# A windowed attention with a SoLU layer: the row scale only in the halves of s, a fixed order on VectorE, a shared transpose of the last 64 columns, x first of the loads

## The chip, the cores and the metric

The kernel runs on one core of a Trainium2 chip. The core has five engines that run side by side, each through its own queue in order: TensorE (PE, with its weight loads as PEld), VectorE (DVE), ScalarE (ACT), GpSimd (POOL) and SyncE (SP, which here only issues DMAs). The metric is the device time in microseconds (us); lower is better. Matmuls write to PSUM, from which DVE and ACT read; POOL works in SBUF alone.

## The reference

Two stages run one after the other. The first is an attention over a window of 7 tokens whose weights are given: a softmax over the 7 taps, then a weighted sum of the current token and the 6 before it, separately for 8 heads of 24 columns. The second is a layer with a SoLU activation and a layer norm, on each of the 8 × 4160 = 33280 tokens:

```
w = exp(weight_gen - max_k)
w = w / (sum_k w + 1e-9)                          # 33280 tokens x 8 heads x 7 taps
x = sum_k w[..., k] * x_pad[t + k]                # 33280 x 192

h = x @ w_in                                      # 192 -> 1024
e = exp(h - max(h))
solu = h * e / (sum(e) + 1e-9)
ln = (solu - mean(solu)) / sqrt(var(solu) + 1e-6) * g_ln
out = ln @ w_out                                  # 1024 -> 192
```

A factor per row that multiplies solu cancels in the layer norm, apart from the small 1e-6; the kernel makes use of that.

## The kernel before

**Tiling.** The tokens are laid out so that each of the 128 partitions owns a run of 260 consecutive tokens; "tile t" is token t of every partition, so a tile is 128 tokens and there are 260 tiles. `starts` cuts the run into chunks (4, 8 and 4 tiles, then 16 each) for the loads, and attention works on groups of 4 tiles (the first two groups have 2).

**The stages of a tile**, with the names that the order uses:

- `att` (`attend`, `attention`): POOL multiplies x by the tap weights (tile `pr`) and adds the seven products partly, leaving two or three partial sums in `half` (`rows_left`). `fin` (`last_sum`) adds the rest on DVE into `a`, and `dup` (`copy_columns`) has ACT copy columns 128 to 191 once more, so that each token has 256 columns in `a`.
- For a pair of tiles, `xT` (`transpose_x`) transposes with four matmuls against the identity into one PSUM tile `pa`: columns 0 to 127 of each token, and columns 128 to 191, twice over, of each token. The first product works with x as a sum of a rounded part and its rest, so `xhi` (`high_x`) rounds `pa` on ACT, `xn` (`subtract_high`) subtracts the rounded part in PSUM with two matmuls against `minus` (the second subtracts only in the lower 64 rows), and `xlo` (`low_x`) copies the rest. For one pair of four (`on_vector`) `xld` (`low_x_on_vector`) has DVE do this in place of `xn` and `xlo`.
- `mm1` (`first_product`) is h = x w_in, ten matmuls into one of three PSUM tiles `h`: three terms with the 128 leading rows and two with the last 64, where the rounded part and its rest fill 128 rows.
- `max`, `vb`, `vr` on DVE: the negated row maximum, a bound that is no less than half of one, and its reciprocal (the row scale SIGMA). `exp` on ACT gives e and its row sum Z. `solu` on DVE writes h × SIGMA × e over h, with the row sum M. `sq` on ACT gives the sum of the squared deviations. `hi` and `lo` write s = h × 2^14 as two half-precision parts (ACT, then DVE), `tr` transposes both with a DMA from SP, and `mm2` (`second_product`) multiplies them with w_out in 24 matmuls. `out` scales on ACT, and `od` stores four tiles at a time.
- `f0` to `f7` (`scales`) work out the last row factor for a group of four tiles by small steps that alternate between ACT and DVE: f0 adds 1e-9 to Z, f1 multiplies by SIGMA, f2 squares, and f3 to f7 form the reciprocal root.
- `t0` to `t6` (`softmax_taps`) are the softmax over the taps of a chunk, on DVE, POOL and ACT in turn.

**The preparation.** w_in and w_out come as 64-bit numbers and are turned into pairs of shorter ones by steps on DVE, ACT and PE (`a..`, `b..` for w_in, `c..`, `q..`, `p..` for w_out), in PSUM tiles that the loop needs later. SP issues the loads of weight_gen's first chunk, then of x's first chunk (L79) and its eight halos (L81), the second weight_gen chunk, w_out, g and x's second chunk; ACT's queue issues the four loads of w_in.

**What sets the order.** All operations of all tiles are put in one order by a planner at build time. `plan` lists each operation with its engine, an assumed duration and what it waits for; `issue_order` plays this through and takes, on each free engine, the operation with the least tile number plus an offset from the table URGENCY, among those that are ready within PATIENCE. Some entries have a `ready` time, before which they aren't placed. The result is a fixed instruction stream for each engine: at run time an engine stands still when its next instruction isn't ready, even if one behind it is.

Of the kernel before, what the change touches and what calls it, by code (L numbers as in the profile page):

```python
# [29 lines left out]
def tile_kernel(ctx: ExitStack, tc: tile.TileContext, x, weight_gen, w_in, w_out, g_ln, out):  # L30
# [39 lines left out]
    def load_x(c, part=0):  # L70
# [5 lines left out]
        if c == 0:  # L76
# [3 lines left out]
            for b in range(B):  # L80
                nc.sync.dma_start(  # L81
                    xv[b * PB + 1 : (b + 1) * PB, :HALO, :],
                    x_run[b * PB : (b + 1) * PB - 1, RUN - HALO :, :],
                )
# [102 lines left out]
    minus = const.tile([P, 2, P], F32R, name="minus")  # L187
    nc.vector.tensor_scalar_mul(minus[:, 0], ident, -1.0)
    nc.vector.tensor_scalar_mul(minus[:D2, 1], ident[:D2], 0.0)
    nc.vector.tensor_scalar_mul(minus[D2:, 1], ident[D2:], -1.0)  # L190
# [197 lines left out]
    def columns(t):  # L388
        return a_of[t // TG][:, t % TG : t % TG + group(t), :]

    def last_sum(t):
        if t % TG == 0:

            a_of[t // TG] = att.tile([P, TG, 2 * P], F32, name="a", bufs=3)
        half = half_of.pop(t)
        nc.vector.tensor_reduce(  # L396
            columns(t)[:, :, :D], half.rearrange("p j t d -> p t d j"), axis=AX.X, op=ALU.add
        )

    def copy_columns(t):  # L400
        a = columns(t)
        nc.scalar.copy(a[:, :, D:], a[:, :, P:D])
# [4 lines left out]
    def transpose_x(t):  # L407
        a = a_of[t // TG]
        pa = ps_a.tile([P, 2, 2, P], F32, name="pa")

        for i in range(2):
            for n in range(2):
                nc.tensor.matmul(  # L413
                    pa[:, n, i, :], a[:, (t + i) % TG, n * P : (n + 1) * P], ident,
                    is_transpose=True, start=i == n == 0, stop=i == n == 1,
                )
        x_parts[t] = [pa]

    def high_x(t):
        hi = small.tile([P, 2, 2, P], F32R, name="x_hi", bufs=2)  # L420
        nc.scalar.copy(hi, x_parts[t][0])  # L421
        x_parts[t].append(hi)

    def subtract_high(t):

# [1 line left out]
        for n in range(2):
            nc.tensor.matmul(
                pa[:, n], minus[:, n], hi[:, n], start=False, stop=n == 1, skip_group_check=True
            )  # L430

    def low_x(t):
        pa, hi = x_parts.pop(t)
        lo = small.tile([P, 2, 2, P], F32R, name="x_lo", bufs=2)
        nc.scalar.copy(lo, pa)  # L435
        for i in range(2):
            xt_of[t + i] = hi[:, 0, i, :], lo[:, 0, i, :], lo[:, 1, i, :]

    def low_x_on_vector(t):

        pa, hi = x_parts.pop(t)
        lo = small.tile([P, 2, 2, P], F32R, name="x_lo", bufs=2)
        for out, n, rows in ((lo, 0, slice(None)), (hi, 1, slice(D2, P))):
            nc.vector.tensor_tensor(
                out=out[rows, n], in0=pa[rows, n], in1=hi.bitcast(F32)[rows, n], op=ALU.subtract
            )
        for i in range(2):
            xt_of[t + i] = hi[:, 0, i, :], lo[:, 0, i, :], hi[:, 1, i, :]
# [41 lines left out]
    def solu(t):  # L490
        h, e = h_of[t], e_of[t]
        nc.vector.scalar_tensor_tensor(  # L492
            out=h, in0=h, scalar=stat(t, SIGMA), in1=e, op0=ALU.mult, op1=ALU.mult, accum_out=stat(t, M)
        )
# [8 lines left out]
    def high_half(t):  # L503
        hl = hl_of[t] = big.tile([P, 2, FF], F16, name="hl", bufs=3)
        nc.scalar.activation(hl[:, 0, :], h_of[t], AF.Copy, scale=2.0**14)  # L505

    def low_half(t):
        hl = hl_of[t]
        nc.vector.scalar_tensor_tensor(  # L509
            out=hl[:, 1, :], in0=h_of[t], scalar=2.0**14, in1=hl[:, 0, :],  # L510
# [10 lines left out]
    def scales(t, step):  # L521
# [9 lines left out]
        if step == 0:  # L531
            nc.scalar.activation(of(ZE), of(Z), AF.Copy, bias=1e-9)
        elif step == 1:
            reduce(U, ZE, 2, ALU.mult)
        elif step == 2:
            nc.scalar.activation(of(E), of(U), AF.Square, scale=1e-3 * FF**1.5)
# [363 lines left out]
```

## Time and profile before

| | us |
|---|---|
| median of 3 runs | 1310.42 |
| lowest and highest run | 1307.23, 1311.84 |
| the profiled execution | 1309.91 |
| its span, first to last instruction | 1308.1 |

The granted TensorE clock of the profiled execution is 0.994 over the span. The costliest groups of each engine, by source line:

| line | engine | what | count | busy us | mean ns |
|---|---|---|---|---|---|
| L135 | POOL | products of taps and x, four tiles | 64 | 621.5 | 9711 |
| L561 | PE | second product | 6192 | 557.4 | 247 |
| L492 | DVE | solu | 260 | 333.5 | 1283 |
| L509 | DVE | second half of s | 260 | 317.7 | 1222 |
| L473 | DVE | row maximum | 260 | 316.8 | 1218 |
| L498 | ACT | squares | 260 | 293.7 | 1130 |
| L413 | PE | transposes of x | 520 | 80.4 | 276 |
| L428 | PE | subtraction of the rounded part | 196 | 47.2 | 322 |

Busy time is the time in which at least one instruction of the group runs. Instructions of one engine overlap at their ends, so the mean duration is longer than the step from one start to the next. The first product starts at 27.96 us, since its first transposes wait for the first `fin`, which starts at 24.22.

### The profile page before, as it was taken

What the parts mean: (1) busy time and instruction counts of PE and PEld (TensorE: products, weight loads), DVE (VectorE), ACT (ScalarE), POOL (GpSimd) and SP (SyncE); (2) the same over time, 40 slices, a digit from 0 to 9 for tenths busy, and PEclk for the clock granted to TensorE, in tenths of its full rate; (3) what the DMA queues carried; (4) which work ended last, traced back from release to release, by engine and by line L of the source; (5) the groups of instructions that cost most, each with busy time, mean ns of one, the idle gap of its engine ahead of it and who ended that gap; (6) DMA issues with size and microseconds to landing.
All of it is one profiled execution on the core that took longest, in us unless ns stands there. A gap on an engine that the chain in (4) does not pass through costs nothing.

```text
span 1308.1 us, 25825 instructions
## 1 busy us (share of the span) xinstructions
PE 1239.4 (95%) x9574; PEld 1069.3 (82%) x9574; DVE 1247.9 (95%) x2055; ACT 1151.4 (88%) x2271; POOL 1195.8 (91%) x243
## 2 busy tenths in 40 slices
PE   1689999999999999999999999999999999999998
PEld 1577788788888888888888888888888888888887
DVE  6889999999999999999999999999999999999995
ACT  5778888899899989989898989989898998998896
POOL 6999989999999999999999999999999999999910
PEclk9899999999999999999999999999999999999999
DMA  8488658697787969777796987788797876975665
GB/s 236 87 184 181 144 130 175 136 203 140 165 174 144 212 127 204 140 174 167 151 205 132 199 143 167 170 162 189 137 203 141 176 165 141 199 140 119 132 139 130
DMA packets 565917, 211.35 MB, mean 162 GB/s; under 512 B 544552, under 2 KB 545960, under 8 KB 565792
## 3 DMA queue, kind: packets, MB, share of 16 engines
q1 hardware_dynamic: 565344, 208.14, 76.3%
q10 hardware_dynamic: 448, 1.57, 0.5%
q8 instruction: 75, 1.23, 0.4%
q14 instruction: 50, 0.41, 0.1%
HBM read 46.15 MB, written 25.56 MB: 55 GB/s over the span
## 4 chain that ended last, share of the span: by engine, by line
DVE 51%; ACT 24%; issue 16%; PE 7%; DMA 2%; ACTq 0%; SPq 0%; DVEq 0%
DVE h L492 19%; DVE stats L473 15%; ACT e L486 9%; DVE a L396 8%; ACT e L498 5%; ACT hl L505 5%; PE h L459 3%; PE po L561 3%; ACT x_hi L421 2%; DVE hl L509 2%; ACT ot L572 2%; DVE stats L477 2%; DVE wm L114 1%; DVE wm L122 1%; DVE stats L529 1%
## 5 line engine op out<-in xcount | busy, mean ns | idle before, releaser
L135 POOL TENSOR_TENSOR pr<-xt,wt 128x5376 f32<-128x5376 f32 (+1 forms) x66 | 631.4, 9567 | 10.2 <-DMA wt<-in_weight_gen_dram 7.5
L561 PE MATMUL po<-w_hl,hlT 128*128 128x192 f16 x6192 | 557.4, 247 | 13.6 <-ACT ot L572 11.7
L561 PEld LDWEIGHTS <-hlT 128*128 128x128 f16 x6240 | 513.9, 98 | 61.6 <-issue 55.4
L492 DVE SCALAR_TENSOR_TENSOR h<-h,stats,e 128x1024 f32<-128x1024 f32 x260 | 333.5, 1283 | 4.5 <-ACT e L486 4.4
L509 DVE SCALAR_TENSOR_TENSOR hl<-h,hl 128x1024 f16<-128x1024 f32 x260 | 317.7, 1222 | 6.6 <-ACT e L498 2.9
L473 DVE TENSOR_REDUCE stats<-h 128x1 f32<-128x1024 f32 x260 | 316.8, 1218 | 3.7 <-PE h L459 3.0
L486 ACT ACTIVATE e<-h,stats 128x1024 f32<-128x1024 f32 x260 | 292.2, 1124 | 19.1 <-DVE stats L473 10.4
L498 ACT ACTIVATE e<-h,stats 128x1024 f32<-128x1024 f32 x260 | 293.7, 1130 | 7.0 <-DVE hl L509 5.7
L505 ACT ACTIVATE hl<-h 128x1024 f16<-128x1024 f32 x260 | 266.7, 1027 | 25.3 <-DVE h L492 23.4
L459 PE MATMUL h<-wb,x_lo 128*128 128x512 f32 x784 | 216.2, 397 | 0.0
L459 PE MATMUL h<-wa_hi,x_hi 128*128 128x512 f32 x520 | 180.3, 428 | 18.1 <-ACT e L498 10.7
L459 PEld LDWEIGHTS h<-wb,x_lo 128*128 128x128 f32 x784 | 148.6, 190 | 35.7
L147 POOL TENSOR_TENSOR pr<-pr 128x2304 f32<-128x2304 f32 (+1 forms) x34 | 169.6, 4987 | 2.7
L142 POOL TENSOR_TENSOR half<-pr 128x2304 f32<-128x2304 f32 x32 | 164.1, 5128 | 2.5
L459 PE MATMUL h<-wa_hi,x_lo 128*128 128x512 f32 x520 | 164.9, 398 | 1.4 <-ACT x_lo L435 1.4
L459 PE MATMUL h<-wa_lo,x_hi 128*128 128x512 f32 x520 | 164.0, 396 | 0.8 <-DVE wa_lo L268 0.8
L396 DVE TENSOR_REDUCE a<-half 128x768 f32<-128x2304 f32 (+1 forms) x66 | 149.1, 2259 | 0.4
L572 ACT ACTIVATE ot<-po,stats 128x192 f32<-128x192 f32 x258 | 110.7, 429 | 9.5 <-PE po L561 7.6
L459 PEld LDWEIGHTS h<-wa_hi,x_lo 128*128 128x128 f32 x520 | 98.3, 189 | 24.9 <-ACT x_lo L435 1.8
L459 PEld LDWEIGHTS h<-wa_lo,x_hi 128*128 128x128 f32 x520 | 98.3, 189 | 23.7 <-DVE wa_lo L268 1.6
L149 POOL TENSOR_TENSOR half<-pr 128x1536 f32<-128x1536 f32 (+1 forms) x34 | 114.8, 3377 | 2.7
L413 PE MATMUL pa<-ident,a 128*128 128x128 f32 x520 | 80.4, 276 | 27.6 <-DVE a L396 25.2
(77 smaller groups left out, 1132.7 us busy)
## 6 DMA issues: line engine op xcount, KB each, us to landing
out_dram<-ot SPq DMA_DIRECT2D x65, 384.0 KB, 3.4
xt<-in_x_dram SPq DMA_DIRECT2D x30, 576.0 KB, 4.7
xt<-in_x_dram SPq DMA_DIRECT2D x30, 480.0 KB, 4.5
wt<-in_weight_gen_dram SPq DMA_DIRECT2D x15, 448.0 KB, 4.5
hlT<-hl SPq DMA_TRANSPOSE x260, 4.3
hlT<-in_moe_w_out_dram SPq DMA_DIRECT2D x4, 384.0 KB, 5.4
xt<-in_x_dram SPq DMA_DIRECT2D x3, 384.0 KB, 5.1
hlT<-in_moe_w_in_dram ACTq DMA_DIRECT2D x2, 512.0 KB, 9.2
```

The costliest lines, as they stand in the source:

```text
L135: nc.gpsimd.tensor_tensor(out=window(pr, 0, [(TG * D, K), (HG, n * H), (1, HG)]), in0=window(xt, t * D, [(D, K), (HG, n * H), (1, HG)]), i ...
L142: nc.gpsimd.tensor_tensor(out=half, in0=pr[:, :3], in1=pr[:, 3:6], op=ALU.add)
L147: nc.gpsimd.tensor_tensor(out=pr[:, :3], in0=pr[:, :3], in1=pr[:, 3:6], op=ALU.add)
L396: nc.vector.tensor_reduce(columns(t)[:, :, :D], half.rearrange("p j t d -> p t d j"), axis=AX.X, op=ALU.add)
L459: nc.tensor.matmul(h[:, fs], lhs, rhs[:, fs], start=n == 0, stop=n == len(terms) - 1)
L473: nc.vector.tensor_reduce(stat(t, NMAX), h_of[t], axis=AX.X, op=ALU.max, negate=True)
L486: nc.scalar.activation(e, h_of[t], AF.Exp, bias=stat(t, NMAX), accum_out=stat(t, Z))
L492: nc.vector.scalar_tensor_tensor(out=h, in0=h, scalar=stat(t, SIGMA), in1=e, op0=ALU.mult, op1=ALU.mult, accum_out=stat(t, M))
L498: nc.scalar.activation(e_of.pop(t), h_of[t], AF.Square, bias=stat(t, M), scale=-float(FF), accum_out=stat(t, Q),)
L505: nc.scalar.activation(hl[:, 0, :], h_of[t], AF.Copy, scale=2.0**14)
L509: nc.vector.scalar_tensor_tensor(out=hl[:, 1, :], in0=h_of[t], scalar=2.0**14, in1=hl[:, 0, :], op0=ALU.mult, op1=ALU.subtract,)
L561: nc.tensor.matmul(po[:, :D], hlT[:, half * NJ + j, :], w2_hl[:, j, w, :], start=n == 0, stop=n == len(terms) - 1,)
```

## The change

- **Row scale only in the halves.** solu multiplies by a constant (`BOOST`, 2^10) where it multiplied by SIGMA; `hi` and `lo` multiply by SIGMA where they multiplied by 2^14. The statistics are therefore of the unscaled solu: f0 and f1 go, f2 squares Z with its small addend as a bias (`least`), and f7 multiplies by SIGMA as a third factor. The slots of `stats` are reordered so that the factors are neighbours, and the constant in `prepare_second` takes up the new power of two.
- **Fixed order on VectorE.** From tile 4 on (`FIXED`), `turn` adds links that hold DVE's five large and small steps to one sequence: max(t+1), lo(t), vb(t+1), solu(t+1), vr(t+1), then max(t+2). Other DVE work is placed between them by the planner as before.
- **One block for the last 64 columns of a pair.** `a` has, for two tokens, three blocks of 128 columns: each token's first 128, and the last 64 of both side by side. `fin` becomes two reductions, `dup` goes, and the pair is transposed by three matmuls. ACT rounds all three blocks (`xhi`), copies the rounded last rows of the second token to a fourth block (`xh2`), and PE subtracts with one matmul of 384 columns (`xn`) for every pair; `xld` goes. ACT then copies the rest of the two first blocks (`xlo`) and, with a shift by 64 partitions, the rest of the last rows of each token (`xl0`, `xl1`). The tiles `x_hi` and `x_lo` have three buffers instead of two.
- **x first of the loads.** x's first chunk is issued right behind weight_gen's; its halos alternate between ACT's and SP's queues; w_in's leading rows go half to SP and half to ACT.
- URGENCY, PATIENCE, the `ready` times and some assumed durations are others.

The diff, cut to its core:

```
-                nc.sync.dma_start(
+                queue = nc.sync if b % 2 else nc.scalar
+                queue.dma_start(
                     xv[b * PB + 1 : (b + 1) * PB, :HALO, :],
                     x_run[b * PB : (b + 1) * PB - 1, RUN - HALO :, :],
                 )
...
     load_w(0)
+    load_x(0)
     for f in range(2):
         nc.scalar.dma_start(raw_b[f * D2 : (f + 1) * D2, :], w_in[P:, f * FF : (f + 1) * FF])
-    for f in range(2):
-        nc.scalar.dma_start(raw_a[f], w_in[:P, f * FF : (f + 1) * FF])
+    for f, queue in enumerate((nc.sync, nc.scalar)):
+        queue.dma_start(raw_a[f], w_in[:P, f * FF : (f + 1) * FF])
     nc.scalar.preload_act_table_set("natural_log_exp_and_others")
-    load_x(0)
     load_w(1)
...
-            nc.vector.tensor_scalar_add(kinv, k, (127 - 73 + 1) << 23)
+            nc.vector.tensor_scalar_add(kinv, k, (127 - 73 + 15) << 23)
...
+        half = half_of.pop(t).rearrange("p r (j i) d -> p j i d r", i=2)
+        a = a_of[t // TG][:, t % TG // 2 :][:, : group(t) // 2]
+        rest = a[:, :, 2].rearrange("p j (i d) -> p j i d", i=2)
+        nc.vector.tensor_reduce(a[:, :, :2], half[..., :P, :], axis=AX.X, op=ALU.add)
+        nc.vector.tensor_reduce(rest, half[..., P:, :], axis=AX.X, op=ALU.add)
...
+        for n in range(3):
+            nc.tensor.matmul(
+                pa[:, n], a[:, n], ident, is_transpose=True, start=n == 0, stop=n == 2,
+            )
...
+    def high_x(t):
+        hi = small.tile([P, 4, P], F32R, name="x_hi", bufs=3)
+        nc.scalar.copy(hi[:, :3], x_parts[t][0])
+    def high_rest(t):
+        nc.scalar.copy(hi[D2:, 3], pa[D2:, 2])
+    def subtract_high(t):
+        nc.tensor.matmul(pa, minus, hi[:, :3], start=False, stop=True, skip_group_check=True)
+    def low_x(t):
+        lo = small.tile([P, 2, P], F32R, name="x_lo", bufs=3)
+        nc.scalar.copy(lo, pa[:, :2])
+            xt_of[t + i] = hi[:, i], lo[:, i], hi[:, 2 + i]
+    def low_rest(t, i):
+        if i == 0:
+            nc.scalar.copy(hi[D2:, 2], pa[:D2, 2])
+        else:
+            nc.scalar.copy(hi[:D2, 3], pa[D2:, 2])
...
-            out=h, in0=h, scalar=stat(t, SIGMA), in1=e, op0=ALU.mult, op1=ALU.mult, accum_out=stat(t, M)
+            out=h, in0=h, scalar=BOOST, in1=e, op0=ALU.mult, op1=ALU.mult, accum_out=stat(t, M)
...
-        nc.scalar.activation(hl[:, 0, :], h_of[t], AF.Copy, scale=2.0**14)
+        nc.scalar.activation(hl[:, 0, :], h_of[t], AF.Copy, scale=stat(t, SIGMA))
...
-            out=hl[:, 1, :], in0=h_of[t], scalar=2.0**14, in1=hl[:, 0, :],
+            out=hl[:, 1, :], in0=h_of[t], scalar=stat(t, SIGMA), in1=hl[:, 0, :],
...
-        if step == 0:
-            nc.scalar.activation(of(ZE), of(Z), AF.Copy, bias=1e-9)
-        elif step == 1:
-            reduce(U, ZE, 2, ALU.mult)
-        elif step == 2:
-            nc.scalar.activation(of(E), of(U), AF.Square, scale=1e-3 * FF**1.5)
+        if step == 2:
+            nc.scalar.activation(of(E), of(Z), AF.Square, bias=least, scale=EPSILON)
...
-            reduce(OUT, Y2, 2, ALU.mult)
+            reduce(OUT, Y2, 3, ALU.mult)
...
-    for part, at in (("b", 7500), ("a0", 8000), ("a1", 8500), *((f"c{f}", 13000) for f in range(4))):
+    for part, at in (("b", 10000), ("a0", 12000), ("a1", 13500), *((f"c{f}", 18000 + 1500 * f) for f in range(4))):
...
-            add(f"t{k}", t, engine, busy, more, *after, ready=(3000, 8000)[c] if c < 2 and k == 0 else 0)
+            add(f"t{k}", t, engine, busy, more, *after, ready=(3500, 17000)[c] if c < 2 and k == 0 else 0)
...
-        add("att", t, POOL, part * (16850 if three else 18480), 60, *after, ready=12000 if c == 1 else 7500)
+        add("att", t, POOL, part * (16850 if three else 18480), 60, *after, ready=8500)
...
+    def turn(name, t):
+        return [(name, t, -9999)] if FIXED <= t < run else []
...
+        add("max", t, DVE, 1131, 84, ("mm1", t), ("exp", t - 4), *turn("vr", t - 1))
+        add("vb", t, DVE, 62, 84, ("max", t), ("f7", stats_of[t - 24] if t >= 24 else -1, -9999), *turn("lo", t - 1))
+        add("vr", t, DVE, 80, 83, ("vb", t), *turn("solu", t))
+        add("solu", t, DVE, 1200, 89, ("exp", t), *turn("vb", t))
+        add("hi", t, ACT, 904, 120, ("solu", t), ("vr", t), ("tr", t - 3))
+        add("lo", t, DVE, 1131, 90, ("hi", t), *turn("max", t + 1))
```

More of the change, by code (lines that the diff above doesn't have):

```diff
@@ L186, in tile_kernel @@
     sq = const.tile([P, 4], F32, name="sq")
[L187 to L190, printed above, removed]
+    minus = const.tile([P, P], F32R, name="minus")
+    nc.vector.tensor_scalar_mul(minus, ident, -1.0)
     middle = const.tile([P, 1], F32, name="middle")
@@ L386, in attend @@
         attention(xs[c], ws[c], t - starts[c], n, half)
-    def columns(t):
-        return a_of[t // TG][:, t % TG : t % TG + group(t), :]
     def last_sum(t):
         if t % TG == 0:
[L394 to L402, printed above, removed]
+            a_of[t // TG] = att.tile([P, TG // 2, 3, P], F32, name="a", bufs=3)
@@ L405, in tile_kernel @@
+        half = half_of.pop(t).rearrange("p r (j i) d -> p j i d r", i=2)
[3 more added lines that the diff above has]
+        nc.vector.tensor_reduce(rest, half[..., P:, :], axis=AX.X, op=ALU.add)
     x_parts = {}
     def transpose_x(t):
[L408 to L416, printed above, removed]
+        a = a_of[t // TG][:, t % TG // 2]
@@ L417, in transpose_x @@
+        pa = ps_a.tile([P, 3, P], F32, name="pa")
+        for n in range(3):
+            nc.tensor.matmul(
+                pa[:, n], a[:, n], ident, is_transpose=True, start=n == 0, stop=n == 2,
+            )
         x_parts[t] = [pa]
     def high_x(t):
-        hi = small.tile([P, 2, 2, P], F32R, name="x_hi", bufs=2)
-        nc.scalar.copy(hi, x_parts[t][0])
+        hi = small.tile([P, 4, P], F32R, name="x_hi", bufs=3)
+        nc.scalar.copy(hi[:, :3], x_parts[t][0])
         x_parts[t].append(hi)
+    def high_rest(t):
+        pa, hi = x_parts[t]
+        nc.scalar.copy(hi[D2:, 3], pa[D2:, 2])
@@ L424, in subtract_high @@
     def subtract_high(t):
         pa, hi = x_parts[t]
[L427 to L430, printed above, removed]
+        nc.tensor.matmul(pa, minus, hi[:, :3], start=False, stop=True, skip_group_check=True)
     def low_x(t):
-        pa, hi = x_parts.pop(t)
-        lo = small.tile([P, 2, 2, P], F32R, name="x_lo", bufs=2)
-        nc.scalar.copy(lo, pa)
+        pa, hi = x_parts[t]
@@ L436, in low_x @@
+        lo = small.tile([P, 2, P], F32R, name="x_lo", bufs=3)
+        nc.scalar.copy(lo, pa[:, :2])
         for i in range(2):
[L437 to L448, printed above, removed]
+            xt_of[t + i] = hi[:, i], lo[:, i], hi[:, 2 + i]
@@ L462, in first_product @@
         h_of[t] = h
-    ZE, SIGMA, Q, E, Y, V, Y2, R, OUT, M, Z, U, L, T, NMAX, HALF, BOUND = range(17)
-    stats = const.tile([P, 6, TG, 17], F32, name="stats")
+    Q, E, Y, V, Y2, R, BOUND, OUT, M, Z, L, T, NMAX, HALF, SIGMA = range(15)
+    stats = const.tile([P, 6, TG, 15], F32, name="stats")
+    EPSILON = 1e-3 * FF**1.5 * BOOST
+    least = const.tile([P, 1], F32, name="least")
+    nc.gpsimd.memset(least, EPSILON * 1e-9)
     nc.gpsimd.memset(stats[:, :, :, HALF], 0.5)
@@ L605, in tile_kernel @@
             ops[f"p{n}{half}"] = once(prepare_second, n, half)
+    for n in range(2):
+        ops[f"xl{n}"] = lambda t, n=n: low_rest(t, n)
     for n in range(LOADS):
         ops[f"lx{n}"] = at_chunk(load_x, n)
-    for n in range(8):
+    for n in range(2, 8):
         ops[f"f{n}"] = at(scales, n)
@@ L611, in tile_kernel @@
         ops[f"t{n}"] = at_chunk(softmax_taps, n)
-    for op, t in issue_order(plan(RUN, starts, group, stat_group, rows_left, on_vector, LOADS)):
+    for op, t in issue_order(plan(RUN, starts, group, stat_group, rows_left, LOADS)):
         ops[op](t)
 URGENCY = {
[15 rows of a table removed]
[14 rows of a table added]
 }
-PATIENCE = (119, 122, 167, 1430, 1765)
+PATIENCE = (83, 294, 305, 1430, 4113)
 PE, DVE, ACT, SP, POOL = range(5)
@@ L648, with plan @@
 }
-def plan(run, starts, group, stat_group, rows_left, on_vector, loads):
+FIXED = 4
+def plan(run, starts, group, stat_group, rows_left, loads):
     hop = {
@@ L767, in plan @@
         after += [("mm1", run - 1), ("out", t - 2)] if t >= run - 4 else [("out", t - 1)]
-        add("mm2", t, PE, 1923, 218, ("tr", t), *after)
+        add("mm2", t, PE, 1930, 218, ("tr", t), *after)
         add("out", t, ACT, 303, 125, ("mm2", t), ("f7", stats_of[t]), ("od", t // 4 * 4 - 5))
@@ L771, in plan @@
             tiles = range(t - n + 1, t + 1)
-            add("f0", t, ACT, 97, 116, *(("exp", u, -160) for u in tiles))
-            add("f1", t, DVE, 70, 87, ("f0", t), *(("vr", u) for u in tiles))
-            add("f2", t, ACT, 97, 116, ("f1", t))
+            add("f2", t, ACT, 97, 116, *(("exp", u, -160) for u in tiles))
             add("f3", t, DVE, 70, 87, ("f2", t), *(("sq", u) for u in tiles))
```

37 lines of the change are left out of this document (14 added, 23 removed), and 29 rows, old and new, of the table URGENCY.

## The prediction

> **What bounds the kernel now.** I read the page's busy times first, then its chain of work that ended last, both for the whole span.
>
> ```profile
> PE 1239.4 (95%) x9574; PEld 1069.3 (82%) x9574; DVE 1247.9 (95%) x2055; ACT 1151.4 (88%) x2271; POOL 1195.8 (91%) x243
> DVE 51%; ACT 24%; issue 16%; PE 7%; DMA 2%; ACTq 0%; SPq 0%; DVEq 0%
> ```
>
> Four engines lie close together, and the chain runs through DVE for half of the span. An average hides stages, so next come the windows, cut where every eighth POOL group begins (32 tiles each); the columns are the length, then PE, PEld, DVE, ACT and POOL busy, clock, DMA share and GB/s.
>
> ```profile
> core 0: us, PE busy (x) PEld busy (x) DVE busy (x) ACT busy (x) POOL busy (x), PEclk, DMA share, GB/s
> 327.64:479.11 151.47, 150.57 (x1177) 130.30 (x1175) 149.73 (x247) 138.45 (x272) 146.74 (x29) 1.00 0.80 168
> ...
> 782.70:934.21 151.51, 150.63 (x1178) 130.39 (x1176) 149.76 (x247) 138.59 (x273) 146.78 (x30) 1.00 0.80 167
> sum 606.57, PE 602.86 PEld 521.72 DVE 599.25 ACT 554.13 POOL 587.05; mean PE 150.72 PEld 130.43 DVE 149.81 ACT 138.53 POOL 146.76
> ```
>
> The middle of the run repeats every 32 tiles: 606.57 / 128 = **4.74 us a tile**. PE is busy for 99.4% of it, DVE for 98.8%, POOL for 96.8%, ACT for 91.4%. PE and DVE both have almost no air, so a gain has to lower both. Whether their busy time is real work is read from the timeline of DVE (start, duration):
>
> ```profile
> 656.40 1.21 DVE L473 TENSOR_REDUCE stats<-h 128x1 f32<-128x1024 f32 x1
> 657.53 1.07 DVE L114 TENSOR_REDUCE wm<-wt 128x128 f32<-128x896 f32 x1
> 658.52 0.14 DVE L477 TENSOR_REDUCE stats<-stats 128x1 f32<-128x2 f32 x1
> 658.59 0.15 DVE L529 TENSOR_REDUCE stats<-stats 128x4 f32<-128x8 f32 x1
> ...
> 661.12 1.22 DVE L473 TENSOR_REDUCE stats<-h 128x1 f32<-128x1024 f32 x1
> 662.38 0.16 DVE L477 TENSOR_REDUCE stats<-stats 128x1 f32<-128x2 f32 x1
> 662.57 0.16 DVE L482 RECIPROCAL stats<-stats 128x1 f32<-128x1 f32 x1
> 662.65 1.23 DVE L509 SCALAR_TENSOR_TENSOR hl<-h,hl 128x1024 f16<-128x1024 f32 x1
> 663.79 1.28 DVE L492 SCALAR_TENSOR_TENSOR h<-h,stats,e 128x1024 f32<-128x1024 f32 x1
> 664.99 0.14 DVE L492 DVE_READ_ACCUMULATOR h<-h,stats,e 128x1 f32 x1
> ```
>
> DVE's busy time holds gaps. Behind an instruction that it does not depend on, the next one starts early: max (L473) to L114 takes 1.13 us, L477 to L529 0.07. Where the next one reads the result, it starts late: max to the bound (L477) takes 1.26, the bound to the reciprocal (L482) 0.19. So the dependent order max, bound, reciprocal costs 0.13 + 0.12 = 0.25 us where nothing is put between. The same reading on PE:
>
> ```profile
> 703.82 0.49 PE L428 MATMUL pa<-x_hi,minus 128*128 128x256 f32 x2
> 704.15 0.62 PE L459 MATMUL h<-wa_hi,x_hi 128*128 128x512 f32 x2
> ...
> 710.82 0.60 PE L413 MATMUL pa<-ident,a 128*128 128x128 f32 x4
> 711.25 2.14 PE L561 MATMUL po<-w_hl,hlT 128*128 128x192 f16 x24
> 713.18 0.48 PE L428 MATMUL pa<-x_hi,minus 128*128 128x256 f32 x2
> ...
> 716.46 2.15 PE L561 MATMUL po<-w_hl,hlT 128*128 128x192 f16 x24
> 718.40 0.70 PE L459 MATMUL h<-wa_hi,x_hi 128*128 128x512 f32 x2
> 720.81 1.41 PE L561 MATMUL po<-w_hl,hlT 128*128 128x192 f16 x15
> ```
>
> From start to start: second product 1.94, first product 2.41, four transposes 0.43, the two subtractions 0.33. Per tile that is 1.94 + 2.41 + (0.43 + 0.75 × 0.33) / 2 = 4.69 us, three pairs of four having the subtraction on PE. Of the 4.74 only 0.05 is waiting: PE is a real limit.
>
> **PE, part by part.** A pair now has three transposes for four: 0.43 × 3/4 = 0.32. One subtraction of 384 columns takes the place of two of 256: 0.33 × 384/512 = 0.25, bounded by 0.17 (one of the two) and 0.33. But every pair has it, also the one in four that DVE did. Per tile (0.32 + 0.25) / 2 = 0.285 instead of 0.34. PE's floor goes from 4.69 to **4.63**.
>
> **DVE.** These groups, the two waits (us in all, times, longest) and one ACT pair carry the rest of the working:
>
> ```profile
> L396 DVE TENSOR_REDUCE a<-half 128x768 f32<-128x2304 f32 x32 | 89.8, 2805 | 0.0
> L396 DVE TENSOR_REDUCE a<-half 128x768 f32<-128x1536 f32 x32 | 57.4, 1793 | 0.4
> L444 DVE TENSOR_TENSOR x_hi<-pa,x_hi 64x256 fp32r<-64x256 f32 x32 | 13.7, 427 | 0.5
> L444 DVE TENSOR_TENSOR x_lo<-pa,x_hi 128x256 fp32r<-128x256 f32 x32 | 13.3, 415 | 0.2 <-ACT x_hi L421 0.2
> L486 ACT ACTIVATE e<-h,stats 128x1024 f32<-128x1024 f32 x260 | 292.2, 1124 | 19.1 <-DVE stats L473 10.4 <-DVE stats L477 0.4
> L505 ACT ACTIVATE hl<-h 128x1024 f16<-128x1024 f32 x260 | 266.7, 1027 | 25.3 <-DVE h L492 23.4 <-DVE stats L529 0.4
> L421 ACT CAST x_hi<-pa 128x512 fp32r<-128x512 f32 x130 | 76.6, 589 | 4.2 <-PE pa L413 2.1 <-PE h L459 1.8
> L402 ACT COPY a<-a 128x256 f32<-128x256 f32 x64 | 25.6, 400 | 8.9 <-DVE a L396 8.7
> ACT stats L536 <- DVE stats L529: 33.0, 33, 2.2
> POOL wt L128 <- DVE stats L482: 19.2, 11, 2.8
> ...
> 720.45 0.59 ACT L435 CAST x_lo<-pa 128x512 fp32r<-128x512 f32 x1
> 720.92 1.14 ACT L498 ACTIVATE e<-h,stats 128x1024 f32<-128x1024 f32 x1
> ```
>
> - Removed: the two subtractions (L444), (0.427 + 0.415) / 8 = 0.10 a tile, and the statistics step f1, some 0.09 per four tiles, 0.02.
> - Moved: the fixed order runs max(t+1), lo(t), bound(t+1), solu(t+1), reciprocal(t+1). No neighbour reads its neighbour's result, so a tile needs 1.13 + 1.14 + 0.07 + 1.20 + 0.08 = 3.62 where the quoted tile (661.12 to 664.99) took 3.87.
> - Added: last_sum is two reductions over the same elements: between 0.07 (a small instruction's step) and 0.16 (its whole duration) per four tiles, 0.02 to 0.04 a tile. I take 0.03.
> - The per-row factor leaves solu and enters lo. L492 steps 1.20 and L509 1.14, and I cannot tell from them whether the factor or the accumulation is dear; the sum is 0 to +0.06, and I take 0.
>
> With last_sum's (2.81 + 1.79 − 2 × 0.1) / 8 = 0.55, 0.03 for its second half, three tap steps of about 0.95 per 16 tiles (0.18) and three statistics steps (0.07) DVE needs **4.45 us** a tile against 4.68 busy now. It stops being a bound. [...]
>
> **ACT.** Between 1024 and 512 columns L505 and L421 differ by 0.438, so 0.86 ns a column, and the next instruction starts 0.47 behind a 512-column one (720.45 to 720.92): a step of 0.03 + 0.86 ns × columns. The five pieces of a pair (384, 128, 256, 128, 128 columns) step 0.36 + 0.14 + 0.25 + 0.14 + 0.14 = 1.03, or 0.52 a tile. Before: 1.75 × 0.47 / 2 = 0.41, and L402 0.28 / 4 = 0.07. No row has ACT on 64 lanes or shifted ones; on DVE 64 lanes cost as much as 128 (427 and 415 ns), which I take over; the bounds are 0.09 (a statistics step) and 0.28 (L402) for one piece. f0 goes (−0.03). The first half's factor becomes per-row: L486, with a per-row bias and an accumulation, takes 0.10 more than L505 for the same columns; bounds 0 and 0.10, and I take 0.10. In sum +0.11: ACT goes from 554.13 / 128 = 4.33 to 4.44. [...] The removed f1 also takes with it the 33.0 us that ACT stood before f2 (L536) with the x pieces and squares queued behind.
>
> **POOL** is untouched: 587.05 / 128 = 4.59 us a tile and about 0.08 behind each of 28 instructions, so 4.66. It lost the rest, 0.08, in L128 behind DVE's reciprocal, which should shrink as DVE gets there sooner. After the change PE (4.63) and POOL (4.66) are the limits, and the small waits don't all go. I take **4.675**: 0.06 less for each of the 256 tiles from tile 4 on, 15.4 us. The bounds are 4.66 (20 us) and 4.705, half (8 us).
>
> **Start.** The rows:
>
> ```profile
> 1.82 8.54 SPq L81 DMA_DIRECT2D xt<-in_x_dram  x8
> 14.30 4.94 POOL L135 TENSOR_TENSOR pr<-xt,wt 128x2688 f32<-128x2688 f32 x1 [7.49 <-DMA wt<-in_weight_gen_dram]
> 14.35 0.62 DVE L114 TENSOR_REDUCE wm<-wt 128x64 f32<-128x448 f32 x1 [5.08 <-DMA wt<-in_weight_gen_dram]
> 4.00:8.00 4.00, 0.00 (x0) 0.00 (x0) 0.91 (x4) 1.15 (x4) 1.15 (x2) 1.00 1.03 234
> ```
>
> POOL's first product starts at 14.30, about 4 us after SP has issued the eighth halo load (1.82 + 8.54 = 10.36). With four on each queue the last is issued at about 6.1, so 4.3 sooner; but the transfers were saturated by then (DMA share 1.03), and ACT issues its four halos ahead of the weights and of its first exponential, which comes late. I take 3 us; bounds 0 and 5. The weights land some 4 us later, which costs DVE its early start, but the tap step that blocked DVE for 5.08 us is due later (17.0 for 8.0 in the plan), which gives that back. The queue order (w_in's first half behind the halos on SP, the w_out loads behind it) is covered by this. Tail: nothing touched.
>
> **Sum**, against the profiled execution's 1309.91 us (span 1308.1; 0.5 below the median of 1310.42): 1309.9 − 15.4 − 3 = **1291.5 us**.
>
> **The rivals.**
> - *DVE or POOL keeps the rate at 4.705* since waits between the engines come back in other places: 1309.9 − 3 − 0.03 × 256 = 1299. For it: POOL's floor is 4.66 and its waits have stood at 0.08. Against: PE's and DVE's work both fall.
> - *x lands no sooner and the weights later*: the first product keeps its time and the start loses 2 us: 1309.9 + 2 − 15.4 = 1296.5. [...]
> - *The ramp shrinks too*: POOL's group of tile 64 begins at 327.64, 313.3 after the first; 64 tiles at 4.74 are 303.4. With slack on DVE these 10 us go: 1281.5. For it: POOL's waits behind DVE; against: the w_out preparation still holds h banks.
> - *Slower: the fixed order blocks DVE behind ACT.* lo(t) waits for hi(t), which is 0.10 longer and now waits for the reciprocal; bound, solu, reciprocal and the next max are queued behind lo, and PE waits for their h bank. DVE has 4.68 − 4.45 = 0.23 us a tile of cover; if ACT is late by more on average, DVE is slower than now. ACT late by 0.37: 4.45 + 0.37 = 4.82, so 1309.9 − 3 + 0.08 × 256 = 1327. For it: ACT gets fuller, with five x pieces instead of two; its waits show it arriving late. Against: max(t+1) (1.13) covers most of hi (1.03), and the longest cause of ACT's waits goes.
>
> **Chances.** Forecast 0.50 (own range 1285 to 1297), waits come back 0.18, start 0.10, ramp 0.10, slower 0.12. A range from 1280 to 1306 leaves out the slower case and the tails of the others. A difference of 0.3% (4 us) is about what a measurement of this kernel can tell from none: faster than that 0.82 (the first four but for 0.06 of the two rivals that gain least), within 0.07 (those 0.06 and 0.01 of the slower case), slower 0.11.
>
> **What would show it.** Right: about 4.675 us a tile in the windows, PE at 99%, DVE's busy share well below 98.8%, max followed by lo at 1.13; three transposes at about 0.32 and one 384-column subtraction at 0.25; L536 no longer among the waits; the first POOL product at about 11. Wrong: DVE idle before lo or solu, released by ACT, with PE idle behind it; L128's waits grown; ACT pieces of 128 columns stepping at 0.25 or more; the first POOL product still at 14.

## The result, and the profile after

| | before | after |
|---|---|---|
| median, us | 1308.83 | 1353.84 |
| lowest, highest | 1306.39, 1311.84 | 1351.34, 1355.96 |
| profiled execution, its span | 1309.91, 1308.1 | 1354.59, 1352.8 |
| row maximum of tile 64 starts at | 368.41 | 370.16 |
| row maximum of tile 224 starts at | 1126.12 | 1158.13 |
| a tile between the two | 4.736 | 4.925 |
| row maximum of the last tile starts at | 1288.17 | 1330.13 |

The change makes the kernel slower: the ratio is 1.0342, with an interval from 1.0311 to 1.0373, 45 us where a gain of 18 was forecast. The table says where: up to tile 64 the two kernels stand within 2 us of each other, and from there each tile takes 0.19 us more, which is 30 us up to tile 224. Another 10 us come up to the last tile, since the kernel before gets faster there and the changed one doesn't. So it is the rate, and hardly the start or what follows the last row maximum (under 3 us). First the page's busy times, then the windows cut every 32 tiles (first of five, and their sum):

```profile
PE 1255.0 (93%) x9378; PEld 1048.7 (78%) x9378; DVE 1191.7 (88%) x1988; ACT 1234.7 (91%) x2560; POOL 1196.0 (88%) x244
```

```profile
370.16:527.75 157.59, 152.80 (x1155) 127.75 (x1154) 143.58 (x241) 148.56 (x309) 153.43 (x31) 1.00 0.79 161
...
sum 787.97, PE 763.85 PEld 638.64 DVE 717.90 ACT 742.71 POOL 740.56; mean PE 152.77 PEld 127.73 DVE 143.58 ACT 148.54 POOL 148.11
```

DVE went from 98.8% to 91.1% busy (717.90 of 787.97), as the change intends, but nobody got its time: PE fell from 99.4% to 96.9%, and ACT, which had been the least loaded at 91.4%, is at 94.3%. (The page's chain is of no use here: it covers 1% of this span.) The waits of the changed kernel, from the views of the single engines (us in all, times, longest):

```profile
PE h L445 <- ACT e L487: 36.4, 63, 3.3
...
DVE hl L498 <- ACT hl L494: 88.2, 147, 2.0
DVE hl L498 <- ACT e L487: 26.9, 45, 1.4
...
ACT stats L533 <- DVE stats L518: 27.4, 34, 1.5
...
POOL wt L131 <- DVE wy L129: 43.5, 12, 6.8
```

Most of the new waiting leads to ACT: VectorE's lo (L498) stands 115 us for ACT's hi and squares, where its counterpart L509 before the change waited some 6; TensorE's first product waits for the squares, which free an h bank; POOL's tap step waits longer (43.5 us, for 27.5 before) for a VectorE that waits itself. So what does ACT do with its time? Its timeline around the pieces of one pair of tiles (start, duration):

```profile
723.86 0.46 ACT L411 CAST x_hi<-pa 128x384 fp32r<-128x384 f32 x1
724.33 0.26 ACT L416 CAST x_hi<-pa 64x128 fp32r<-64x128 f32 x1
724.61 1.11 ACT L487 ACTIVATE e<-h,stats 128x1024 f32<-128x1024 f32 x1
...
727.80 0.43 ACT L557 ACTIVATE ot<-po,stats 128x192 f32<-128x192 f32 x1
728.25 0.26 ACT L434 CAST x_hi<-pa 64x128 fp32r<-64x128 f32 x1
728.53 0.26 ACT L432 CAST x_hi<-pa 64x128 fp32r<-64x128 f32 x1
728.80 0.37 ACT L425 CAST x_lo<-pa 128x256 fp32r<-128x256 f32 x1
729.06 1.12 ACT L487 ACTIVATE e<-h,stats 128x1024 f32<-128x1024 f32 x1
```

Read the starts against the durations. The wide copy L425 lasts 0.37, and the next instruction starts 0.26 behind it: neighbours overlap by 0.11. But L411 lasts 0.46, and L416 starts 0.47 behind it; L416 lasts 0.26 and is followed at 0.28, L434 at 0.28, L432 at 0.27. Around each copy that begins at partition 64 on its input or its output side the overlap is gone, and the instruction behind such a copy also starts only when it has ended. The pair has five such places: into L416, out of it, into L434, from there to L432, and out of L432. The five pieces step 0.47 + 0.28 + 0.28 + 0.27 + 0.26 = 1.56 us, where the prediction had 1.03, and the scaling of the output, L557, ahead of them takes longer too (0.45 to the next start where it takes about 0.31 elsewhere). The whole trace has it so: nothing overlaps into L416, out of it, from L434 to L432 or from L432 to L425 (117 to 130 neighbours each, median steps 0.47, 0.29, 0.27 and 0.27 for durations of 0.46, 0.26, 0.26 and 0.26). L434 overlaps with the instruction ahead of it only behind the small L533 (12 of 130, a step of 0.30 for a duration of 0.40).

### The profile page after: what moved, and what is told of

Its sections match the earlier page's. It is cut to its first block, busy times and chain, and to the rows that moved or that the text cites. A ratio compares the mean times of both kernels' runs of the same rounds, so it can differ in the third digit from the quotient of the medians.

```text
span 1352.8 us, 25541 instructions
## 1 busy us (share of the span) xinstructions
PE 1255.0 (93%) x9378; PEld 1048.7 (78%) x9378; DVE 1191.7 (88%) x1988; ACT 1234.7 (91%) x2560; POOL 1196.0 (88%) x244
## 5 line engine op out<-in xcount | busy, mean ns | idle before, releaser
L498 DVE SCALAR_TENSOR_TENSOR hl<-h,stats,hl 128x1024 f16<-128x1024 f32 x260 | 333.2, 1282 | 116.7 <-ACT hl L494 88.2
L481 DVE SCALAR_TENSOR_TENSOR h<-h,e 128x1024 f32<-128x1024 f32 x260 | 317.8, 1223 | 0.7 <-ACT e L475 0.7
L462 DVE TENSOR_REDUCE stats<-h 128x1 f32<-128x1024 f32 x260 | 313.2, 1205 | 5.6 <-PE h L445 5.6
L494 ACT ACTIVATE hl<-h,stats 128x1024 f16<-128x1024 f32 x260 | 288.9, 1111 | 4.6 <-DVE stats L471 2.8
L445 PE MATMUL h<-wb,x_hi 128*128 128x512 f32 x1040 | 285.8, 396 | 0.0
L445 PEld LDWEIGHTS h<-wb,x_hi 128*128 128x128 f32 x1040 | 195.9, 188 | 48.1
L445 PE MATMUL h<-wa_hi,x_hi 128*128 128x512 f32 x520 | 187.3, 441 | 36.4 <-ACT e L487 36.4
L557 ACT ACTIVATE ot<-po,stats 128x192 f32<-128x192 f32 x258 | 108.6, 421 | 38.2 <-PE pa L404 16.3
L445 PEld LDWEIGHTS h<-wa_hi,x_hi 128*128 128x128 f32 x520 | 79.2, 190 | 68.3 <-ACT e L487 54.2
L393 DVE TENSOR_REDUCE a<-half 128x512 f32<-128x1536 f32 (+1 forms) x66 | 103.3, 1565 | 0.0
```

Source lines behind the costliest of these rows:

```text
L445: nc.tensor.matmul(h[:, fs], lhs, rhs[:, fs], start=n == 0, stop=n == len(terms) - 1)
L462: nc.vector.tensor_reduce(stat(t, NMAX), h_of[t], axis=AX.X, op=ALU.max, negate=True)
L481: nc.vector.scalar_tensor_tensor(out=h, in0=h, scalar=BOOST, in1=e, op0=ALU.mult, op1=ALU.mult, accum_out=stat(t, M))
L494: nc.scalar.activation(hl[:, 0, :], h_of[t], AF.Copy, scale=stat(t, SIGMA))
L498: nc.vector.scalar_tensor_tensor(out=hl[:, 1, :], in0=h_of[t], scalar=stat(t, SIGMA), in1=hl[:, 0, :], op0=ALU.mult, op1=ALU.subtract,)
```

## The experiments

Theory A: ScalarE has too much to do, and its late results hold VectorE up. Theory B: the fixed sequence is at fault, whatever ScalarE has to do. After the first four runs, theory C: what makes ScalarE's work too much is the late start around each change of the start partition; theory D: small or 64-lane copies are dear by themselves. Each time stands beside the kernel before on the same chip; "rate" is the mean step from the row maximum of tile 64 to that of tile 224, in us a tile.

| run | median us | ratio to before, interval | rate |
|---|---|---|---|
| before | 1308.83 | | 4.736 |
| the change | 1353.84 | 1.0342 [1.0311, 1.0373] | 4.925 |
| e1, no fixed sequence | 1498.87 | 1.1454 [1.1432, 1.1476] | 5.509 |
| e2, small copies on all lanes | 1303.07 | 0.996 [0.9945, 0.9976] | 4.729 |
| e3, constant in hi | 1334.83 | 1.0204 [1.0186, 1.0222] | 4.851 |
| e4, e2 and e3 | 1285.44 | 0.9823 [0.9806, 0.984] | 4.657 |
| e5, rests at partition 0 | 1299.23 | 0.9917 [0.9902, 0.9932] | 4.709 |
| e6, rests at partition 64 | 1326.67 | 1.0127 [1.0112, 1.0142] | 4.818 |
| e7, one copy wide | 1337.42 | 1.0208 [1.0191, 1.0225] | 4.858 |
| e8, only the loads | 1310.99 | 1.0011 [1.0, 1.0022] | 4.738 |
| e9, same work, new order | 1348.94 | 1.0311 [1.0296, 1.0327] | 4.909 |
| e10, e7 with a new order | 1332.73 | 1.0186 [1.0169, 1.0203] | 4.862 |
| e11, e10 without the sequence | 1324.38 | 1.0125 [1.011, 1.014] | 4.796 |
| e12, shift by DMA | 1297.47 | 0.9907 [0.9891, 0.9924] | 4.756 |

**e1: without the fixed sequence.**

```
     def turn(name, t):
-        return [(name, t, -9999)] if FIXED <= t < run else []
+        return []
```

> The changed kernel without the fixed sequence on VectorE (the links between max, lo, bound, solu and reciprocal are gone; all else, work and tables, is kept). Theory A (ScalarE has too much to do for any order: its steps sum to 4.60 us a tile against 4.18 before): the steady rate stays at 4.85 to 5.0 us a tile, time 1340 to 1370. Theory B (the fixed sequence itself blocks VectorE behind ScalarE): back to 4.75 or less, 1310 or less.

1498.87 us, outside both expectations. The table of offsets was made for the sequence, and without it the planner's order is bad on all engines: between tiles 64 and 224 VectorE and ScalarE each waited 0.71 us a tile, and TensorE 0.63. The granted clock was lower as well (0.959, for 0.994 in the changed kernel); no run here shows why. It doesn't tell A from B; e11 asks the question again.

**e2: the small copies on all lanes.**

```
-        nc.scalar.copy(hi[D2:, 3], pa[D2:, 2])
+        nc.scalar.copy(hi[:, 3], pa[:, 2])
...
-            nc.scalar.copy(hi[D2:, 2], pa[:D2, 2])
+            nc.scalar.copy(hi[:, 2], pa[:, 2])
-            nc.scalar.copy(hi[:D2, 3], pa[D2:, 2])
+            nc.scalar.copy(hi[:, 3], pa[:, 2])
```

> Order kept, but the three small copies of the last rows work on all 128 partitions from partition 0 with the same 128 columns, so there is no shift and the last rows of x are not the reference's. If a change of the start partition makes ScalarE's next instruction wait for the end of the one before, their steps fall from 0.26 to 0.29 us to about 0.15 and that of the 384-column copy from 0.47 to 0.36, some 0.24 us a tile less. Theory A: the rate falls by 0.15 to 0.2, time 1300 to 1320. Theory B: time above 1340. If the small copies have a dear fixed part of their own, the steps stay at 0.25 or more.

1303.07 us: 51 us gone with the same number of instructions, the same columns, the same order and twice the lanes. ScalarE's timeline:

```profile
708.36 0.46 ACT L411 CAST x_hi<-pa 128x384 fp32r<-128x384 f32 x1
708.72 0.27 ACT L416 CAST x_hi<-pa 128x128 fp32r<-128x128 f32 x1
...
711.69 0.27 ACT L434 CAST x_hi<-pa 128x128 fp32r<-128x128 f32 x1
711.83 0.29 ACT L432 CAST x_hi<-pa 128x128 fp32r<-128x128 f32 x1
711.99 0.41 ACT L425 CAST x_lo<-pa 128x256 fp32r<-128x256 f32 x1
```

The small copies step 0.14 to 0.16 us, the 384-column copy 0.36. Theory B falls as the main cause: the fixed sequence is in this kernel.

**e3: a constant in hi.**

```
-        nc.scalar.activation(hl[:, 0, :], h_of[t], AF.Copy, scale=stat(t, SIGMA))
+        nc.scalar.activation(hl[:, 0, :], h_of[t], AF.Copy, scale=2.0)
```

> Order kept; the first half of s is scaled by a constant instead of the per-row factor (the second half is not, so the output is not the reference's). The step of that instruction falls from 1.00 to 0.91 us if the per-row operand is what costs. Theory A: 0.07 to 0.1 us a tile less, 1330 to 1338. Theory B: within 6 us of the changed kernel.

1334.83 us, 19 less, as theory A had it; the instruction steps 0.90 where it stepped 1.00. (With these inputs the row's factor is 2 in every row, since no row maximum reaches the bound's half of one; so nothing is left out after all.)

**e4: both.**

> The two edits of e2 and e3 together: ScalarE's steps sum to about 4.27 us a tile, near those of the kernel before, under the fixed sequence. Theory A: faster than the kernel before, 4.66 to 4.72 a tile, 1288 to 1303. Theory B: still above 1325.

1285.44 us, 2% under the kernel before and a little below theory A's range. The gains add up (51 + 19 = 70, measured 68). Its windows from 358 to 1100 us, their sum:

```profile
sum 742.00, PE 737.35 PEld 633.73 DVE 712.43 ACT 696.92 POOL 733.38; mean PE 368.67 PEld 316.87 DVE 356.22 ACT 348.46 POOL 366.69
```

PE is at 99.4% again (737.35 of 742.00) and POOL at 98.8%: with ScalarE relieved of both, TensorE and POOL are the limits, as the prediction wanted.

But the kernel that the prediction priced is e2 and not e4: its sum had the five pieces at 1.03 us a pair (1.08 in e2) and the per-row factor at 0.10 on top. With these costs the rate is 4.729, only 0.007 below the kernel before; taking the factor off ScalarE brings it to 4.657. The waits in e2, then in e4:

```profile
DVE hl L498 <- ACT hl L494: 60.6, 144, 3.1
DVE hl L498 <- ACT e L487: 10.9, 20, 1.2
...
PE h L445 <- ACT e L487: 17.3, 35, 2.9
...
DVE hl L498 <- ACT hl L494: 46.0, 140, 1.6
DVE hl L498 <- ACT e L487: 8.7, 19, 1.2
...
PE h L445 <- ACT e L487: 10.0, 19, 2.7
```

So 0.07 of the factor's 0.10 us a tile reaches the rate even when the copies are cheap. What e2 gains on the kernel before, it has by tile 64, whose row maximum starts at 357.69 for 368.41.

**e5 and e6: the same two copies at partition 0 and at partition 64.** In both the copy of the rounded last rows is on all lanes. e5, then e6:

```
-            nc.scalar.copy(hi[D2:, 2], pa[:D2, 2])
+            nc.scalar.copy(hi[:D2, 2], pa[:D2, 2])
-            nc.scalar.copy(hi[:D2, 3], pa[D2:, 2])
+            nc.scalar.copy(hi[:D2, 3], pa[:D2, 2])
...
-            nc.scalar.copy(hi[D2:, 2], pa[:D2, 2])
+            nc.scalar.copy(hi[D2:, 2], pa[D2:, 2])
-            nc.scalar.copy(hi[:D2, 3], pa[D2:, 2])
+            nc.scalar.copy(hi[D2:, 3], pa[D2:, 2])
```

> Order kept; the copy of the rounded last rows works on all 128 partitions, the two small copies of the rests read and write partitions 0 to 63 (64 lanes, no instruction of ScalarE in the loop starts elsewhere; the last rows of x are not the reference's). Theory C (a start partition other than the one before makes the next instruction wait for the end of this one): steps of 0.15 us for both, time as with all lanes, 1300 to 1306. Theory D (64 lanes or the small copies as such are dear): steps of 0.26 or more for the two rests, 1320 to 1340.

> As e5, but the two rests read and write partitions 64 to 127 (last rows not the reference's). Theory C: the first of the two starts late and so does the instruction behind the second, but the step from the first to the second is 0.15 us, so two late starts a pair, 0.1 us a tile more than e5: 1315 to 1328. If any start at 64 is dear by itself, both step by 0.26 or more.

ScalarE's timeline in e5:

```profile
709.56 0.25 ACT L434 CAST x_hi<-pa 64x128 fp32r<-64x128 f32 x1
709.70 0.27 ACT L432 CAST x_hi<-pa 64x128 fp32r<-64x128 f32 x1
709.86 0.38 ACT L425 CAST x_lo<-pa 128x256 fp32r<-128x256 f32 x1
710.13 1.12 ACT L487 ACTIVATE e<-h,stats 128x1024 f32<-128x1024 f32 x1
```

and in e6:

```profile
704.15 0.26 ACT L434 CAST x_hi<-pa 64x128 fp32r<-64x128 f32 x1
704.31 0.26 ACT L432 CAST x_hi<-pa 64x128 fp32r<-64x128 f32 x1
704.59 0.37 ACT L425 CAST x_lo<-pa 128x256 fp32r<-128x256 f32 x1
```

64 lanes are not the cost: in e5 they step 0.14 and 0.16. Nor is partition 64: in e6 the second of two copies that both begin there follows the first after 0.16. The change is the cost: from L432 back to a copy at partition 0 takes 0.28. One side is enough: in the changed kernel L434 differs from L557 ahead of it in the partition of its output alone (0.45 for 0.31), and L425 from L432 in that of its input alone (0.27). The durations (0.25 to 0.27) are the same in both; only the overlap differs. 1299.23 us is a little better than theory C's 1300, 1326.67 within its range; theory D falls.

**e7: one copy wide**, the first edit of e2 alone; the upper half that it writes is overwritten later by the shifted rest, so that nothing is left out.

> Order kept, and nothing left out: the copy of the rounded last rows works on all 128 partitions (the upper half is overwritten later by the shifted rest), the two rests shift as in the changed kernel. Theory C: two late starts of five a pair go, the 384-column copy steps 0.36 and the next 0.16, 0.11 us a tile less of ScalarE: 1326 to 1338. Theory D with 64 lanes as the cost: only that one copy is cheaper, 1338 to 1346.

1337.42 us, inside theory C's range and just outside theory D's. The steps tell them apart: 0.36 for the 384-column copy and 0.16 for the next, as theory C had it. With five changes of the start partition a pair the time is 1353.8, with three 1337.4 (e7), with two 1326.7 (e6), with none 1299.2 (e5) or 1303.1 (e2): 8 to 14 us for each. By the overlap of 0.11 that is lost, a change is worth an estimated 130 pairs × 0.11 = 14 us on ScalarE, so most of it reaches the end.

**e8: only the loads**, in the kernel before: x's first chunk behind weight_gen's, halos on two queues, w_in's halves on two.

> The kernel before with the new order of the loads and nothing else (its order of operations kept). If x landing sooner carries through: 1304 to 1307. If the later weights set the start: the first product of w_in starts at 30 to 34 us instead of 27.96 and the time is 1311 to 1317. Neither theory of the steady rate says more than that the rate stays at 4.74.

1310.99 us, 1.2 more than before, on the edge of what can be told. Neither expectation holds: the time lies just below the range of the later weights and above that of the sooner x. In e8

```profile
11.23 4.94 POOL L136 TENSOR_TENSOR pr<-xt,wt 128x2688 f32<-128x2688 f32 x1
14.08 0.70 DVE L212 TENSOR_SCALAR h<-hl 128x512 int32<-128x512 int32 x1 [3.58 <-DMA hl<-in_moe_w_in_dram]
...
29.01 1.05 PE L460 MATMUL h<-wa_hi,x_hi 128*128 128x512 f32 x2
```

POOL starts 3.1 us sooner, and the first step of w_in 6.2 us later (14.08 for 7.84); the first product then starts 1.05 us later than before (27.96).

**e9, e10, e11: a new order.** The planner assumed 0.904 for hi and 0.148 for each small copy. Here its assumed steps are set to the measured ones and its tables are searched anew; e9 keeps every instruction, e10 has e7's wide copy, e11 also drops the sequence.

```
-        add("xh2", t, ACT, 148, 115, ("xhi", t, -9999), ("xT", t))
+        add("xh2", t, ACT, 290, 110, ("xhi", t, -9999), ("xT", t))
...
-        add("hi", t, ACT, 904, 120, ("solu", t), ("vr", t), ("tr", t - 3))
+        add("hi", t, ACT, 1000, 120, ("solu", t), ("vr", t), ("tr", t - 3))
```

> The changed kernel with every instruction kept; only the order differs: the planner's assumed steps are set to those measured (hi 1.00, lo 1.20, solu 1.14, the 384-column copy 0.465, the small copies 0.27 to 0.29, f2 0.20) and its tables are searched anew by its own playback; the fixed sequence stays. Theory C with the order planned for wrong steps: ScalarE's work still sums to 4.60 us a tile, but the waits of 0.43 on VectorE shrink; 4.70 to 4.80 a tile, 1300 to 1325. If the amount of ScalarE's work alone sets the time: 1345 or more.

> As e9 with the wide copy of e7 (two late starts of five a pair gone), order planned for its measured steps, fixed sequence kept. 0.11 us a tile less on ScalarE than e9: 1290 to 1312. If order is all: the same as e9.

> As e10 without the fixed sequence on VectorE, the tables searched anew for that. If the fixed sequence itself costs (theory B): faster than e10 by 5 us or more, 1282 to 1300. If the sequence is harmless once the order is planned for the true steps: within 5 us of e10.

e9 gives 1348.94: 5 us of 45. The expectation of 1300 to 1325 was wrong, and the other one, that the amount of ScalarE's work sets the time (1345 or more), fits; this other order helps little. e10 misses its range as well, at 1332.73, but stands 16.2 us below e9, as e7 stood 16.4 below the change: the two late starts are worth the same in both pairs, though e10's tables are others than e9's. e11 is 8.4 us faster than e10, more than the 5 us of theory B, but outside its range of 1282 to 1300. Its tables are others as well, so what the fixed sequence costs by itself isn't shown. How good an order for this work could be stays open too, since only one search was tried for each.

**e12: the shift by DMA.** A repair that leaves nothing out, with the wide copy and a new order:

```
-        lo = small.tile([P, 2, P], F32R, name="x_lo", bufs=3)
-        nc.scalar.copy(lo, pa[:, :2])
+        lo = small.tile([P, 3, P], F32R, name="x_lo", bufs=3)
+        nc.scalar.copy(lo, pa)
...
+        h32, l32 = hi.bitcast(F32), lo.bitcast(F32)
+        nc.sync.dma_start(h32[D2:, 2], l32[:D2, 2])
+        nc.sync.dma_start(h32[:D2, 3], l32[D2:, 2])
```

> A repair that leaves nothing out: as e10, but ScalarE copies the rest of all three blocks in one instruction and SP moves the two 64-row parts to their place with two SBUF-to-SBUF transfers a pair, so no instruction of ScalarE in the loop starts at another partition; tables searched anew by the planner's playback, fixed sequence kept. Theory C: ScalarE's steps for a pair fall to 0.36 + 0.16 + 0.36, 0.44 us a tile instead of 0.81, and the time to 1290 to 1306, below the kernel before. If the transfers come too late for the first product or hold up the transposes behind them on SP, the wait shows on TensorE before the first product or the second, and the time is 1310 or more.

1297.47 us: faster than both kernels (0.9907 of before, interval 0.9891 to 0.9924). Its pieces step 0.36 + 0.16 + 0.36. The rate isn't where it gains: in the profiled execution, the slowest of its five (1303.9), a tile takes 4.756 us, no less than before, but the row maximum of tile 64 starts at 358.24, 10 us sooner. What it still pays, from its waits:

```profile
DVE hl L498 <- ACT hl L494: 48.4, 121, 1.6
...
PE h L445 <- DMA x_hi<-x_lo: 15.7, 15, 2.6
```

## Why the prediction was wrong

**The step that failed** is the sentence on ScalarE's pieces: "No row has ACT on 64 lanes or shifted ones; on DVE 64 lanes cost as much as 128 (427 and 415 ns), which I take over". The durations are indeed the same (0.26 to 0.27). But a copy costs its engine the step to the next start, and for the 128-column pieces I had worked the step out, 0.14, from neighbours that all begin at partition 0. It measured 0.27 to 0.28, at the upper bound that I had named for a piece (0.28), and the 384-column copy ahead of them, for which I had named no bound, stepped 0.47 instead of 0.36. The pair's sum was 1.56 instead of 1.03. The instructions that I took the 427 and 415 ns from show the lost overlap in the trace of before, had I read their starts:

```profile
649.69 0.16 DVE L529 TENSOR_REDUCE stats<-stats 128x4 f32<-128x8 f32 x1
649.76 0.41 DVE L444 TENSOR_TENSOR x_lo<-pa,x_hi 128x256 fp32r<-128x256 f32 x1
650.19 0.43 DVE L444 TENSOR_TENSOR x_hi<-pa,x_hi 64x256 fp32r<-64x256 f32 x1
650.64 1.80 DVE L396 TENSOR_REDUCE a<-half 128x768 f32<-128x1536 f32 x1
```

L529 is overlapped by its successor (0.07 against 0.16); the subtraction at partition 64 starts 0.43 us behind one that lasts 0.41, and its own successor 0.45 behind its start, for a duration of 0.43. All 32 pairs of these subtractions in that trace step so: 0.42 to 0.45 for a duration of 0.41 to 0.42, and 0.44 to 0.46 for one of 0.43. For ScalarE no row of before had the case; in the changed kernel its copies step 0.27 to 0.29 for a duration of 0.26 at such a change.

**What followed from it.** ScalarE is busy for 742.71 / 160 = 4.64 us a tile, where I had 4.44. The rival that came true is the slower one, in its mechanism: lo waits behind ScalarE, and PE behind both. I had put its threshold at 0.23 us of lateness a tile and priced a lateness of 0.37 at 1327. Between tiles 64 and 224 VectorE's wait for lo is 0.41 a tile; by the same rule that is 4.45 + 0.41 = 4.86 and 1338. The rest up to 1354 is VectorE's own work, 717.90 / 160 = 4.49 and not 4.45, and its other waits. The chance of 0.12 was too small because the slack of ScalarE was the thinnest support of the sum: one unseen instruction form, used three times a pair.

**A second step failed behind the first.** The sum took ScalarE's other addition, the per-row factor in hi, to be covered ("max(t+1) (1.13) covers most of hi (1.03), and the longest cause of ACT's waits goes"). Its size was right: 0.10 taken, 0.10 measured as a step (mean 1111 against 1027 ns). But it costs 19 us in the changed kernel (e3) and 18 us with cheap copies (e2 against e4), so it was covered in neither. With the pieces at nearly the price that I gave them (e2) the rate is 4.729 and not 4.675. That e2's 1303 lies within the range of 1280 to 1306 is luck: it gains up to tile 64, and not by the rate that the forecast rested on.

**What held.** TensorE:

```profile
706.03 0.42 PE L420 MATMUL pa<-x_hi,minus 128*128 128x384 f32 x1
706.29 0.71 PE L445 MATMUL h<-wa_hi,x_hi 128*128 128x512 f32 x2
...
713.17 0.49 PE L404 MATMUL pa<-ident,a 128*128 128x128 f32 x3
713.49 2.14 PE L546 MATMUL po<-w_hl,hlT 128*128 128x192 f16 x24
```

three transposes 0.32 and the subtraction 0.26, against 0.32 and 0.25. In e4 the rate is 4.657, close to the forecast's 4.675, but there ScalarE does 0.10 us a tile less than the forecast had. VectorE's gaps went as predicted:

```profile
715.88 1.20 DVE L462 TENSOR_REDUCE stats<-h 128x1 f32<-128x1024 f32 x1
717.00 1.07 DVE L125 TENSOR_REDUCE wm<-wt 128x128 f32<-128x896 f32 x1
...
725.03 1.21 DVE L462 TENSOR_REDUCE stats<-h 128x1 f32<-128x1024 f32 x1
726.85 1.28 DVE L498 SCALAR_TENSOR_TENSOR hl<-h,stats,hl 128x1024 f16<-128x1024 f32 x1 [0.61 <-ACT hl L494]
728.05 0.15 DVE L466 TENSOR_REDUCE stats<-stats 128x1 f32<-128x2 f32 x1
728.12 1.22 DVE L481 SCALAR_TENSOR_TENSOR h<-h,e 128x1024 f32<-128x1024 f32 x1
729.25 0.14 DVE L481 DVE_READ_ACCUMULATOR h<-h,e 128x1 f32 x1
```

the maximum steps 1.12 where it isn't followed by a wait, lo 1.20 and the bound 0.07; what the sequence gained is spent in waits such as the 0.61 before lo. The per-row factor's move on VectorE came out at nothing, as taken: lo steps 1.20 for 1.14 before, and solu 1.14 for 1.20 up to the reading of its sum.

**What was off beside it.** The start: POOL's first product came 3 us sooner, at 11.33, as taken, but the weights came later than I had allowed for, and e8 gives +1.2 us instead of −3 (no run shows the 2 us that the rival on the loads put in). In the changed kernel the first product of w_in starts at 34.73:

```profile
11.33 4.94 POOL L138 TENSOR_TENSOR pr<-xt,wt 128x2688 f32<-128x2688 f32 x1
14.43 0.68 ACT L220 ACTIVATE part<-hl 128x512 int32<-128x512 uint32 x1 [4.22 <-DMA hl<-in_moe_w_in_dram]
...
34.73 1.20 PE L445 MATMUL h<-wa_hi,x_hi 128*128 128x512 f32 x2
```

yet by tile 64 all but 1.75 us of it is made up, so this isn't the loss. The rival on the ramp shows in the kernels with a relieved ScalarE: the row maximum of tile 64 starts 10 to 15 us sooner than before in e2, e4, e5 and e12, though their loads are those of the changed kernel. And removing f1 freed ScalarE of its wait before f2 (33.0 us), as predicted, but other waits grew: that of L557 is 38.2 us (9.5 before), and that of L533, a later step of f2's chain, 27.4 (22.2 before).

## What to carry to other kernels

Price an instruction by the step from its start to its neighbour's, not by its duration, and ask for each new neighbour whether the overlap still exists: here a change of the first partition between two ScalarE instructions cost 0.11 us or a little more, and five of them in every pair of tiles made the difference between 1299 us (e5) and 1354. A shift of rows between partitions on a loaded engine, 1353.8 us here with five changes a pair, is worth trying with few of them (pieces with the same first partition in a row, 1326.7 us in e6, which leaves the shift out; a wide copy where a later one overwrites the surplus, 1337.4 in e7) or on an engine with air, as the DMA in e12 (1297.5, in an order of its own). And where several engines stand above 90%, the work that a change adds to the least loaded of them has to be the best supported number of the sum, since here the order that is fixed at build time passed its lateness on: of 0.10 us more on ScalarE, 0.07 reached the rate (e2 against e4), with ScalarE busy for 94% in e2 (712.55 of the 756.65 us between tiles 64 and 224).
